# Loading and transposing the first x chunk in halves, and moving gate values through DRAM, in a fused attention and FFN kernel

## The chip, the cores and the metric

The kernel runs on one core of a Trainium2 chip. The metric is the device time of one execution in microseconds (us). "Span" is the time from the first to the last instruction of the profiled execution; the device time is 1.7 to 1.9 us longer in nearly all executions. PE is TensorE (its matmuls), DVE is VectorE, ACT is ScalarE, POOL is GpSimd, and SP is SyncE, which only issues DMAs here; ACTq and SPq are DMA issues of those engines.

A ratio is the mean time of one kernel's fast runs over that of the other's of the same rounds. So it is not quite the ratio of the medians that stand beside it.

## The reference, cut to what matters

```python
g = sigmoid((x * gate_w).sum(-1, keepdims=True))     # one gate value per token
a = infini_attention(x, wq, wk, wv, wo, beta)        # 32 heads of 16, four segments of 512 tokens
b = ((relu(x @ W_gate)) * (x @ W_up)) @ W_down       # 1792 hidden features
return g * a + (1 - g) * b
```

x is 2048 x 512 in bf16. Segment s attends within itself and to a memory matrix made from the keys and values of the segments before it. `beta` gives one mixing value per head.

## The kernel before

A Python list scheduler orders about 1400 operations when the program is built. It models the engines with fixed durations and gives every engine one fixed list. On the chip each engine works through its list in order, and waits on semaphores where an operation needs another engine's result. In before SyncE issued nothing from 21.99 to 28.38 us, where a transpose of keys waited for DVE; the loads of x chunk 2 behind it, which read only DRAM and write a place of their own, were issued from 30.96 us on. A tie is broken by random numbers from a seed. So any change of the operations, and any change of the seed, gives another order everywhere.

The parts that the change touches, with cuts marked:

```python
# loads at the start, in this order on two queues
for i, eng in enumerate(("act", "sp", "act", "sp")):          # x tiles: 128 tokens x 512 features each
    load(eng, [f"hT{i}"], V.hT[:, i, :], x0[:, i, :], 1 << 17)
...  # wq, wk, wv in quarters of 128 KB; wq0 and wq2 on act
load("act", ["gwb"], V.gwb[:], gate_w.partition_broadcast(128), 1 << 17)   # gate weight, fifth on act's queue

# constants from beta, on act and dve
cst = [act(... V.eb = exp(V.braw) ...)]
cst.append(dve(... V.romgh = V.eb + 1 ...))
cst.append(dve(... V.epsv = V.romgh * EPS ...))
...  # eight column fills of vaug from romgh

# gate of segment 0: product on pool, sum and exponential on act
for t in range(4):
    pool(... Tn[t % 2] = hT[t] * gwb ...)
    act(... gl[t] = sum of Tn[t % 2] ...)
act(... gexp = exp(gl) ...)
...
# gate values for the attention's layout: 16 small copies per segment
for a in range(4):
    for jj in range(4):
        ... copy gexp[32*a:32*a+32, 4 tokens] to gexpT[32*jj:32*jj+32, ...]   # on dve or act

# the k mask that an attention matmul ("quad") reads: on dve alone in segment 0
Op([("dve", km, 420)] + ([("act", ka, 720)] if s else []), ...)
```

An attention step is a "quad": matmuls of 32 rows into four banks of PSUM, the memory that matmuls write (`psL`), then one ACT exponential of 128 x 2048 elements into `E`. All quads share those banks, so a quad waits for the exponential of the one before it (0.3 us at B0 in before). PE fills the time between with projections and FFN matmuls. `ek` is an exponential for the keys. The first three bursts of quads are called A0, B0 and C below; 14 matmuls for v stand between A0 and B0 in PE's list.

The softmax here doesn't subtract the row's maximum and nothing guards it: scores larger than these inputs give would overflow.

Of the kernel before, what the change touches and what calls it, by code (L numbers as in the profile page):

```python
# [384 lines left out]
def build_kernel(nc, A_x, A_wq, A_wk, A_wv, A_wo, A_beta, W_g, W_u, W_d, gate_w, out):  # L385
    _, S, D = A_x.shape
    F = W_g.shape[1]
    assert D == 512 and S % 512 == 0 and F % 128 == 0
    NSEG, KT, NF, NT = S // 512, D // 128, F // 128, S // 128
    EPS, SCALE = 1e-6, 16 ** -0.5  # L390
    sc = Sched(seed=59)
    T = {}
    with contextlib.ExitStack() as stack:
        for name, shape, dt in plan(S, D, F):
            T[name] = stack.enter_context(nc.sbuf_tensor(name, shape, dt))
        PL = stack.enter_context(nc.psum_tensor("psL", [128, 4, 512], F32))
        PA = [stack.enter_context(nc.psum_tensor(f"psA{i}", [128, 512], F32)) for i in range(4)]
        for st in sc.streams:
            sc.sem[st] = stack.enter_context(nc.semaphore(f"s_{st}"))
        program(sc, nc, T, PL, PA, A_x, A_wq, A_wk, A_wv, A_wo, A_beta, W_g, W_u, W_d, gate_w, out, NSEG, KT, NF, NT, EPS, SCALE)  # L400
        with nc.Block() as block:
            sc.emit(block)
    return sc


def program(sc, nc, T, PL, PA, A_x, A_wq, A_wk, A_wv, A_wo, A_beta, W_g, W_u, W_d, gate_w, out, NSEG, KT, NF, NT, EPS, SCALE):
# [26 lines left out]
    def xt(c):  # L433
        return [f"xT{c}_{kt}" for kt in range(KT)] if c else [f"xT0_{i}" for i in range(4)]
# [6 lines left out]
    for i, eng in enumerate(("act", "sp", "act", "sp")):  # L441
        load(eng, [f"hT{i}"], V.hT[:, i, :], x0[:, i, :], 1 << 17)
    for nm, w, src in (("wq", V.wq, A_wq), ("wk", V.wk, A_wk), ("wv", V.wv, A_wv)):
        for kt in range(KT):
            load("act" if nm == "wq" and kt % 2 == 0 else "sp", [f"{nm}{kt}"], w[:, kt, :], src[kt * 128:(kt + 1) * 128, :], 1 << 17)
# [63 lines left out]
    xps, xcs = [warm(6, 512, 0, 3)], []  # L509
    for i in range(4):  # L510
        def fx(e, i=i):
            for kt in range(KT):
                ins = e.matmul(PL[:, i, kt * 128:(kt + 1) * 128], lhsT=V.hT[:, i, kt * 128:(kt + 1) * 128], rhs=V.ident[:], start=True, stop=True)
            return ins
        xps.append(pe(fx, 430, reads=[f"hT{i}", "ident"], writes=[f"bankL{i}"], name=f"xt{i}"))
        dst = V.xT[:, :, i * 128:(i + 1) * 128]
        srcp = PL[:, i, :].rearrange("q (k t) -> q k t", k=KT)
        if i % 2 == 0:
            xcs.append(dve(lambda e, d=dst, s_=srcp: e.tensor_copy(d, s_), t_dve(512), reads=[f"bankL{i}"], writes=[f"xT0_{i}"], name=f"xc{i}"))
        else:  # L520
            xcs.append(act(lambda e, d=dst, s_=srcp: e.activation(d, s_, ACT.Copy), t_act(512), reads=[f"bankL{i}"], writes=[f"xT0_{i}"], name=f"xc{i}"))
    xps.append(warm(7, 128, 1, 0))
    sc.queue(0, xps)
# [6 lines left out]
    for s2 in range(2):  # L530
        for tt in range(4):
            cst.append(dve(lambda e, s2=s2, tt=tt: e.tensor_copy(V.vaug[:, s2, tt, :, 16], V.romgh[:, :]), 190, reads=["romgh"], writes=[f"vone{s2}_{tt}"], name="vone"))
# [4 lines left out]
    gq = {"pe": [], "act": [], "dve": [], "flex": [], "pool": [], "sp": []}  # L537
    for c in range(NSEG):
        t0, t1 = 4 * c, 4 * c + 4
        gx = V.gexp[:, t0:t1]  # L540
        if c == 0:
            for t in range(4):
                gq["pool"].append(pool(lambda e, t=t: e.tensor_tensor(V.Tn[:, t % 2, :], V.hT[:, t, :], V.gwb[:], ALU.mult), 1250, reads=[f"hT{t}", "gwb"], writes=[f"Tn{t % 2}"], name=f"gml{t}"))  # L543
                gq["act"].append(act(lambda e, t=t: e.activation(V.Tn[:, t % 2, :], V.Tn[:, t % 2, :], ACT.Copy, accum_out=V.gl[:, t:t + 1]), t_act(512, False) + 100, reads=[f"Tn{t % 2}"], writes=[f"Tn{t % 2}", f"gl{t}"], name=f"gad{t}"))
        else:
            for t in range(t0, t1):
                ld = dma("sp", lambda e, t=t: e.dma_start(V.osb[:, 2, :], A_x[0, t * 128:(t + 1) * 128, :]), 1 << 17, writes=["osb2_0", "osb2_1"], name=f"ldxr{t}")
                ld.after = GATE_T[c] + 4000.0 * (t - t0)
                gq["sp"].append(ld)
                gq["dve"].append(dve(lambda e, t=t: e.tensor_tensor_reduce(out=V.osb[:, 2, :], in0=V.osb[:, 2, :], in1=V.gwb[:], scale=1.0, scalar=0.0, op0=ALU.mult, op1=ALU.add, accum_out=V.gl[:, t:t + 1]),  # L550
                                     t_dve(512) + 70, reads=["osb2_0", "osb2_1", "gwb"], writes=["osb2_0", "osb2_1", f"gl{t}"], name=f"gate{t}"))
# [4 lines left out]
        gexpT_r[c] = []  # L556
        for a in range(4):
            for jj in range(4):
                dst = V.gexpT[32 * jj:32 * jj + 32, 16 * c + 4 * a:16 * c + 4 * a + 4]
                gq["flex"].append(sc.add(Op([("dve", lambda e, a=a, dst=dst, t0=t0, t1=t1: e.tensor_copy(dst, V.gexp[32 * a:32 * a + 32, t0:t1]), 200),  # L560
                                             ("act", lambda e, a=a, dst=dst, t0=t0, t1=t1: e.activation(dst, V.gexp[32 * a:32 * a + 32, t0:t1], ACT.Copy), 215)],
                                            reads=[f"gexp{c}"], writes=[f"gexpT{c}_{a}{jj}"], name="gexpT")))
                gexpT_r[c].append(f"gexpT{c}_{a}{jj}")
# [8 lines left out]
    sc.queue(2, gq["flex"])  # L572
# [15 lines left out]
    def proj(s):  # L588
# [3 lines left out]
        def pj(w, col, name, wname, tokmajor=False):  # L592
            ep = Epoch("proj")

            step = 1 if s == 0 and name == "q" and col < 2 else 2
            for k0 in range(0, KT, step):
# [7 lines left out]
                pes.append(pe(fn, mm(512, step), reads=[f"{wname}{kt}" for kt in range(k0, k0 + step)] + xt(s), name=f"{name}{s}_{col}", ep=ep, role="w2" if k0 else "w"))  # L604
            return ep
        for G in range(4):
            ep = pj(V.wq, G, "q", "wq")
            qs = qslot(s, G)
            evs.append(dve(lambda e, ep=ep, qs=qs: e.tensor_copy(V.qT[:, qs, :], A(ep)[:, :]), t_dve(512), writes=[f"qT{qs}"], name=f"qcp{s}_{G}", ep=ep, role="r"))  # L609
# [3 lines left out]
            evs.append(dve(lambda e, ep=ep, G=G: e.tensor_copy(V.kT[:, G, :], A(ep)[:, :]), t_dve(512), writes=[f"kT{G}"], name=f"kcp{s}_{G}", ep=ep, role="r"))  # L613
            for p in range(2):
# [3 lines left out]
                evs.append(sc.add(Op([("dve", km, 420)] + ([("act", ka, 720)] if s else []), reads=[f"kT{G}", "pm"], writes=[f"kp{ks}"], name=f"kmask{s}_{G}_{p}")))  # L618
# [7 lines left out]
        if s == 0:  # L626
            pes = [p for k in "qkv" for p in pes if p.name[0] == k]
            pes[:2 * KT] = [pes[h * KT + kt] for kt in range(KT) for h in range(2)]
        return pes, evs, sbs, acts, sps

    def va(s):
        return [f"va{s % 2}_{tt}" for tt in range(4)] + [f"vone{s % 2}_{tt}" for tt in range(4)]
# [210 lines left out]
    put(pproj=a, dproj=b, dsb=c_, aphi=d, spk=e_)  # L843
# [89 lines left out]
```

## Time and profile before

| | before |
|---|---|
| device time, median of the first 3 runs | 273.07 us |
| span of the profiled execution | 271.2 us |
| PE / DVE / ACT busy | 97% / 76% / 75% |
| first k matmul, A0, B0, C start | 9.82, 13.94, 17.80, 20.83 us |
| last matmul starts | 268.60 us |

The page's first part gives the busy times of the engines:

```profile
PE 263.0 (97%) x2108; PEld 115.1 (42%) x2143; DVE 204.8 (76%) x382; ACT 203.7 (75%) x210; POOL 99.5 (37%) x156
```

The timeline of the start. Columns: start, busy time, engine, line, operation, out<-in, count; in brackets the idle time of that engine before it, and what ended it.

```profile
3.78 1.89 PE L513 MATMUL psL<-ident,hT 128*128 128x128 bf16 x16 [0.22 <-DMA hT<-in_A_x_dram]
...
6.36 3.63 PE L602 MATMUL psA<-xT,wq 128*128 128x512 bf16 x16
...
9.82 3.62 PE L602 MATMUL psA<-xT,wk 128*128 128x512 bf16 x15
...
11.34 0.19 ACT L544 ACTIVATION_READ_ACCUMULATOR Tn<-Tn 128x1 f32 x1
11.43 0.21 ACT L527 ACTIVATE eb<-braw 128x32 f32<-128x32 bf16 x1
11.67 0.24 DVE L528 TENSOR_SCALAR romgh<-eb 128x32 f32<-128x32 f32 x1 [0.96 <-ACT eb L527]
11.84 0.68 DVE L613 CAST kT<-psA 128x512 bf16<-128x512 f32 x1
...
13.55 0.60 DVE L616 TENSOR_SCALAR kp<-kT,pm 128x512 bf16<-128x512 bf16 x2
...
13.94 0.39 PE L698 MATMUL psL<-qT,kp 32*128 32x512 bf16 x4 [0.51 <-DVE kp L616]
```

PE waits 0.51 us for the first k mask. DVE was late with it, because it had waited 0.96 us for `eb`, and `eb` stood on ACT right behind a gate sum.

The chain of waits of the same stretch. Columns: start, length, what the chain passed through.

```profile
2.68 5.68 DMA gwb<-in_gate_w_dram
...
8.51 4.49 POOL Tn L543 x4
...
13.02 0.73 ACT Tn L544 x2
...
14.01 0.20 ACT gexpT L561
...
14.93 1.06 ACT ek L584
15.98 1.77 ACT E L703
17.76 0.05 issue
17.80 0.40 PE psL L698 x8
```

It says what PE's list of waits doesn't. The load of the gate's weight lands at 8.36. POOL's four products follow it, then ACT's sums, the gate copies, an exponential for the keys (`ek`), and only then the first attention exponential. B0 waits for that.

### The profile page before, as it was taken

The page shows a single profiled execution, that of the slowest core. Times are in us where ns is not written, and L with a number is a line of the kernel's source. Part 1 is how long each engine was busy: PE and PEld are TensorE (multiplying, and loading weights), DVE is VectorE, ACT ScalarE, POOL GpSimd, SP SyncE. Part 2 cuts the span into 40 slices and gives each one's busy share as a digit, 9 for nine tenths or more (in the row PEclk, how much of TensorE's full clock was granted, in tenths as well). Part 3 has the DMA queues.
Part 4 walks back from the last instruction along what each step waited for, and adds up shares of the span by engine and source line. Part 5 has one row for each costly group of instructions (what it writes and reads, how often), then busy time and mean ns, then how long its engine had stood idle before and what let it go on. Part 6 is the DMA issues. An engine that isn't in the chain of part 4 may idle for free.

```text
span 271.2 us, 5268 instructions
## 1 busy us (share of the span) xinstructions
PE 263.0 (97%) x2108; PEld 115.1 (42%) x2143; DVE 204.8 (76%) x382; ACT 203.7 (75%) x210; POOL 99.5 (37%) x156
## 2 busy tenths in 40 slices
PE   8989999999999999999999999999999999999996
PEld 4433343444444444444343444343434444344444
DVE  4689988899889799999888887877773547776300
ACT  3499998898989987899768779887776768682122
POOL 5614343454533253643333532333333242421000
PEclk9999999999999999999999999999999999999999
DMA  6999953102200143210001220000012000000011
GB/s 192 331 365 238 237 96 69 29 7 55 55 25 19 31 89 97 60 39 2 0 2 39 62 78 22 19 2 1 2 39 52 27 19 22 0 0 4 0 39 41
DMA packets 31017, 17.01 MB, mean 63 GB/s; under 512 B 20880, under 2 KB 30992, under 8 KB 30992
## 3 DMA queue, kind: packets, MB, share of 16 engines
q1 hardware_dynamic: 30272, 16.01, 23.3%
q10 hardware_dynamic: 720, 0.66, 1.0%
q8 instruction: 17, 0.28, 0.4%
q14 instruction: 8, 0.07, 0.1%
HBM read 9.84 MB, written 2.10 MB: 44 GB/s over the span
## 4 chain that ended last, share of the span: by engine, by line
PE 88%; ACT 2%; DVE 2%; DMA 2%; issue 2%; POOL 2%; ACTq 1%; DVEq 0%; POOLq 0%
PE psA L780 36%; PE psA L819 17%; PE psL L698 9%; PE psA L602 8%; PE psA L724 7%; PE psA L812 5%; PE psA L600 4%; DMA gwb<-in_gate_w_dram 2%; POOL Tn L543 2%; PE psA L672 1%; PE psA L643 1%; ACT E L703 1%; ACTq L439 1%; DVE osb L828 1%; PE psA L659 0%
## 5 line engine op out<-in xcount | busy, mean ns | idle before, releaser
L703 ACT ACTIVATE E<-psL 128x2048 bf16<-128x2048 f32 x80 | 150.0, 1875 | 31.1 <-PE psL L698 30.6
L706 POOL TENSOR_SCALAR_AFFINE_SELECT E<-E 128x512 bf16<-128x512 bf16 x128 | 85.4, 685 | 139.6 <-ACT E L703 139.5
L780 PE MATMUL psA<-xT,wg 128*128 128x512 bf16 x213 | 58.0, 380 | 1.1 <-issue 0.8
L780 PE MATMUL psA<-xT,wu 128*128 128x512 bf16 x217 | 58.4, 380 | 0.6 <-issue 0.3
L819 PE MATMUL psA<-wd,hT 128*128 128x512 bf16 (+2 forms) x233 | 53.0, 367 | 0.8 <-issue 0.8
L791 DVE TENSOR_TENSOR hT<-psA,rl 128x512 bf16<-128x512 f32 x56 | 38.2, 683 | 13.5 <-PE psA L780 12.5
L698 PE MATMUL psL<-qT,kp 32*128 32x384 bf16 (+3 forms) x512 | 31.7, 301 | 0.8 <-DVE kp L616 0.5
L780 PEld LDWEIGHTS psA<-xT,wu 128*128 128x128 bf16 x224 | 20.4, 98 | 25.8 <-issue 3.2
L819 PEld LDWEIGHTS psA<-wd,hT 128*128 128x128 bf16 x238 | 20.9, 98 | 23.8 <-issue 4.0
L780 PEld LDWEIGHTS psA<-xT,wg 128*128 128x128 bf16 x224 | 20.1, 98 | 24.9 <-issue 3.1
L729 DVE STREAM_TRANSPOSE Tn<-psA 128x512 f32<-128x512 f32 x32 | 20.9, 692 | 7.9 <-PE psA L724 7.9
L789 DVE TENSOR_SCALAR rl<-psA 128x512 bf16<-128x512 f32 x30 | 20.6, 688 | 4.0 <-PE psA L780 3.0
L698 PEld LDWEIGHTS psL<-qT,kp 32*128 32x128 bf16 x512 | 8.9, 92 | 34.0 <-ACT E L703 14.0
L788 ACT ACTIVATE rl<-psA 128x512 bf16<-128x512 f32 x26 | 15.5, 595 | 10.3 <-PE psA L780 10.2
L724 PE MATMUL psA<-E,vaug 128*17 128x256 bf16 (+3 forms) x512 | 20.2, 300 | 0.0
L829 ACT ACTIVATE osb<-psA,omg 128x512 bf16<-128x512 f32 (+2 forms) x10 | 6.4, 645 | 13.7 <-PE psA L812 13.1
L812 PE MATMUL psA<-wo,oT 128*128 128x512 bf16 (+2 forms) x64 | 15.9, 366 | 0.3 <-issue 0.2
L602 PE MATMUL psA<-xT,wk 128*128 128x512 bf16 x62 | 15.9, 380 | 0.2 <-DVE ttmp L585 0.2
L602 PE MATMUL psA<-xT,wq 128*128 128x512 bf16 x61 | 15.5, 380 | 0.5 <-issue 0.3
L600 PE MATMUL psA<-wv,xT 128*128 128x512 bf16 x61 | 14.7, 380 | 0.4 <-issue 0.3
L724 PEld LDWEIGHTS psA<-E,vaug 128*17 128x17 bf16 x512 | 10.7, 90 | 9.4 <-issue 2.5
L609 DVE CAST qT<-psA 128x512 bf16<-128x512 f32 x16 | 10.7, 676 | 3.4 <-PE psA L602 3.3
(71 smaller groups left out, 233.0 us busy)
## 6 DMA issues: line engine op xcount, KB each, us to landing
out_dram<-osb SPq DMA_DIRECT2D x15, 128.0 KB, 1.7
wg<-in_B_W_gate_dram SPq DMA_DIRECT2D x8, 224.0 KB, 5.4
wu<-in_B_W_up_dram SPq DMA_DIRECT2D x8, 224.0 KB, 5.7
wd<-in_B_W_down_dram SPq DMA_DIRECT2D x1, 1792.0 KB, 10.5
osb<-in_A_x_dram SPq DMA_DIRECT2D x12, 128.0 KB, 2.0
wk<-in_A_wk_dram SPq DMA_DIRECT2D x4, 128.0 KB, 5.6
wv<-in_A_wv_dram SPq DMA_DIRECT2D x4, 128.0 KB, 4.9
wo<-in_A_wo_dram SPq DMA_DIRECT2D x1, 512.0 KB, 5.0
```

The costliest lines, as they stand in the source:

```text
L600: ins = e.matmul(A(ep)[:, :], lhsT=V.xT[:, kt, tok + col * 128:tok + (col + 1) * 128], rhs=w[:, kt, :], start=(kt == 0), stop=(kt == KT - 1))
L602: ins = e.matmul(A(ep)[:, :], lhsT=w[:, kt, col * 128:(col + 1) * 128], rhs=V.xT[:, kt, tok:tok + 512], start=(kt == 0), stop=(kt == KT - 1))
L698: ins = q.matmul(PL[:, jj, o:o + w], lhsT=V.kp[32 * jj:32 * jj + 32, kslot(s, n), 128 * j:128 * j + 128], rhs=V.qT[32 * jj:32 * jj + 32, q ...
L703: acts.append(act(lambda a, e=e: a.activation(V.E[:, e, :, :], PL[:, :, :], ACT.Exp, scale=SCALE), t_act(2048), reads=[f"bankL{b}" for b i ...
L706: pools.append(pool(lambda g, ap=ap: g.affine_select(out=ap, in_=ap, compare_op=ALU.is_ge, fill=0.0, base=0, pattern=[[0, 4], [1, 128]], c ...
L724: ins = q.matmul(A(ep)[32 * jj:32 * jj + 17, c:512], lhsT=V.vaug[:, s % 2, j, 8 * G + 2 * jj + p, :], rhs=V.E[:, e, jj, o:o + w], start=(j ...
L729: ds.append(dve(lambda e, p=p, ep=eps[p]: e.transpose(V.Tn[:, p, :], A(ep)[:, :]), t_dve(512), writes=[f"Tn{p}"], name=f"tr{s}_{G}_{p}", e ...
L780: ins = e.matmul(A(ep)[:, :], lhsT=w[:, kt, f * 128:(f + 1) * 128], rhs=V.xT[:, kt, c * 512:(c + 1) * 512], start=(kt == 0), stop=(kt == K ...
L789: ("dve", lambda e, ep=eg, r=r: e.tensor_scalar(V.rl[:, r, :], A(ep)[:, :], 0.0, None, ALU.max), t_dve(512))],
L791: evs.append(dve(lambda e, ep=eu, r=r, hs=hs: e.tensor_tensor(V.hT[:, hs, :], A(ep)[:, :], V.rl[:, r, :], ALU.mult), t_dve(512), reads=[f" ...
L812: ins = e.matmul(A(ep)[:, 0:c1 - c0], lhsT=V.oT[:, o0 + G, i * 128:(i + 1) * 128], rhs=V.wo[:, G, c0:c1], start=st_ and G == 0, stop=sp_ a ...
L819: ins = e.matmul(A(ep)[:, 0:c1 - c0], lhsT=V.hT[:, slots[f], i * 128:(i + 1) * 128], rhs=V.wd[:, f, c0:c1], start=st_ and f == f0, stop=sp ...
```

## The change

Its intent is an earlier start: half of x's features are transposed and projected while the other half is loading. It also takes the small copies of gate values off ACT and DVE (64 copies), moves the constants from beta out of the way, turns eight column fills into one, and allows ACT to make the first k masks. The seed is new. The diff, cut to its core:

```diff
-    sc = Sched(seed=59)
+    sc = Sched(seed=178)
-    for i, eng in enumerate(("act", "sp", "act", "sp")):
-        load(eng, [f"hT{i}"], V.hT[:, i, :], x0[:, i, :], 1 << 17)
+    def load_x0(h):
+        for b, eng in ((0, "act"), (2, "sp")):
+            load(eng, [f"xr{b}_{h}"], V.hT[:, XS + b:XS + b + 2, 256 * h:256 * h + 256], x0[:, b:b + 2, 256 * h:256 * h + 256], 1 << 17)
+    for h in range(2):
+        load_x0(h)
+        for kt in (2 * h, 2 * h + 1):
+            load_w("wq", V.wq, A_wq, kt, "act" if kt % 2 == 0 else "sp")
 ...  (warm-up, 4 x 4 transposes and copies become 2 x 4 x 2, fillers between the halves)
+    cst[0].after = 20000.0          # eb
+    cst[2].after = 40000.0          # epsv
-    for s2 in range(2): for tt in range(4): ... V.vaug[:, s2, tt, :, 16] <- V.romgh
+    ... V.vaug[:, :, :, :, 16] <- V.romgh broadcast, one instruction
-        for a in range(4):
-            for jj in range(4): ... copy of gexp to gexpT, 32 partitions x 4
+        gq["sp"].append(dma("sp", ... gscr[c] <- gexp ...))              # write to DRAM
+        grd = dma("sp", ... [gexpT[32*j:32*j+32] <- gscr[c] for j in range(4)] ...)   # four reads
-            step = 1 if s == 0 and name == "q" and col < 2 else 2
+            early = s == 0 and name == "q" and col < 3                   # three q groups interleaved
-  ... ([("act", ka, 720)] if s else []) ...
+  ... ([("act", ka, 720)] if s or G == 0 else []) ...                    # k mask may go to act
```

More of the change, by code (lines that the diff above doesn't have):

```diff
@@ L433, in xt @@
     def xt(c):
-        return [f"xT{c}_{kt}" for kt in range(KT)] if c else [f"xT0_{i}" for i in range(4)]
+        return [f"xT{c}_{kt}" for kt in range(KT)] if c else [f"xT0_{i}_{h}" for i in range(4) for h in range(2)]
+    XS = 16
     lact, lsp = [], []
@@ L440, in program, with load_w @@
     x0 = A_x[0, 0:512, :].rearrange("(i p) d -> p i d", p=128)
-    for i, eng in enumerate(("act", "sp", "act", "sp")):
-        load(eng, [f"hT{i}"], V.hT[:, i, :], x0[:, i, :], 1 << 17)
-    for nm, w, src in (("wq", V.wq, A_wq), ("wk", V.wk, A_wk), ("wv", V.wv, A_wv)):
+    def load_x0(h):
+        for b, eng in ((0, "act"), (2, "sp")):
+            load(eng, [f"xr{b}_{h}"], V.hT[:, XS + b:XS + b + 2, 256 * h:256 * h + 256], x0[:, b:b + 2, 256 * h:256 * h + 256], 1 << 17)
+    def load_w(nm, w, src, kt, eng="sp"):
+        load(eng, [f"{nm}{kt}"], w[:, kt, :], src[kt * 128:(kt + 1) * 128, :], 1 << 17)
+    for h in range(2):
+        load_x0(h)
+        for kt in (2 * h, 2 * h + 1):
+            load_w("wq", V.wq, A_wq, kt, "act" if kt % 2 == 0 else "sp")
+    for nm, w, src in (("wk", V.wk, A_wk), ("wv", V.wv, A_wv)):
         for kt in range(KT):
-            load("act" if nm == "wq" and kt % 2 == 0 else "sp", [f"{nm}{kt}"], w[:, kt, :], src[kt * 128:(kt + 1) * 128, :], 1 << 17)
+            load_w(nm, w, src, kt)
     load("act", ["gwb"], V.gwb[:], gate_w.partition_broadcast(128), 1 << 17)
@@ L507, in warm, with fx @@
         return pe(fn, m * n * (0.834 if k == 0 else 0.5), writes=[f"bankL{b}"], name=f"warm{k}")
-    xps, xcs = [warm(6, 512, 0, 3)], []
-    for i in range(4):
-        def fx(e, i=i):
-            for kt in range(KT):
-                ins = e.matmul(PL[:, i, kt * 128:(kt + 1) * 128], lhsT=V.hT[:, i, kt * 128:(kt + 1) * 128], rhs=V.ident[:], start=True, stop=True)
-            return ins
-        xps.append(pe(fx, 430, reads=[f"hT{i}", "ident"], writes=[f"bankL{i}"], name=f"xt{i}"))
-        dst = V.xT[:, :, i * 128:(i + 1) * 128]
-        srcp = PL[:, i, :].rearrange("q (k t) -> q k t", k=KT)
-        if i % 2 == 0:
-            xcs.append(dve(lambda e, d=dst, s_=srcp: e.tensor_copy(d, s_), t_dve(512), reads=[f"bankL{i}"], writes=[f"xT0_{i}"], name=f"xc{i}"))
-        else:
-            xcs.append(act(lambda e, d=dst, s_=srcp: e.activation(d, s_, ACT.Copy), t_act(512), reads=[f"bankL{i}"], writes=[f"xT0_{i}"], name=f"xc{i}"))
-    xps.append(warm(7, 128, 1, 0))
-    sc.queue(0, xps)
+    xps, xcs = [[warm(7, 512, 0, 3)], []], []
+    for h in range(2):
+        if h == 1:
+            xps[0].append(warm(6, 128, 1, 0))
+        for i in range(4):
+            def fx(e, i=i, h=h):
+                for kt in (2 * h, 2 * h + 1):
+                    ins = e.matmul(PL[:, i, kt * 128:(kt + 1) * 128], lhsT=V.hT[:, XS + i, kt * 128:(kt + 1) * 128], rhs=V.ident[:], start=True, stop=True)
+                return ins
+            xps[h].append(pe(fx, 115 if h else 215, reads=[f"xr{i & 2}_{h}", f"hT{XS + i}", "ident"], writes=[f"bankL{i}"], name=f"xt{i}"))
+            dst = V.xT[:, 2 * h:2 * h + 2, i * 128:(i + 1) * 128]
+            srcp = PL[:, i, 256 * h:256 * h + 256].rearrange("q (k t) -> q k t", k=2)
+            if i % 2 == 0:
+                xcs.append(dve(lambda e, d=dst, s_=srcp: e.tensor_copy(d, s_), t_dve(256), reads=[f"bankL{i}"], writes=[f"xT0_{i}_{h}"], name=f"xc{i}"))
+            else:
+                xcs.append(act(lambda e, d=dst, s_=srcp: e.activation(d, s_, ACT.Copy), t_act(256), reads=[f"bankL{i}"], writes=[f"xT0_{i}_{h}"], name=f"xc{i}"))
     sc.queue(0, [t for t in xcs if t.eng == "dve"])
@@ L529, in program @@
     cst.append(dve(lambda e: e.tensor_scalar(V.epsv[:], V.romgh[:], EPS, None, ALU.mult), 190, reads=["romgh"], writes=["epsv"], name="epsv"))
-    for s2 in range(2):
-        for tt in range(4):
-            cst.append(dve(lambda e, s2=s2, tt=tt: e.tensor_copy(V.vaug[:, s2, tt, :, 16], V.romgh[:, :]), 190, reads=["romgh"], writes=[f"vone{s2}_{tt}"], name="vone"))
+    cst.append(dve(lambda e: e.tensor_copy(V.vaug[:, :, :, :, 16].rearrange("q s t h -> q (s t) h"), V.romgh[:, :].unsqueeze(1).to_broadcast([128, 8, 32])), 420, reads=["romgh"], writes=["vone"], name="vone"))
+    cst[0].after = 20000.0
+    cst[2].after = 40000.0
     sc.queue(0, [t for t in cst if t.eng == "act"])
@@ L536, in program @@
     gexpT_r = {}
-    gq = {"pe": [], "act": [], "dve": [], "flex": [], "pool": [], "sp": []}
+    gscr = nc.dram_tensor("gscr", [NSEG, 4, 32, 4], F32).ap()
+    gq = {"pe": [], "act": [], "dve": [], "pool": [], "sp": []}
     for c in range(NSEG):
@@ L542, in program @@
             for t in range(4):
-                gq["pool"].append(pool(lambda e, t=t: e.tensor_tensor(V.Tn[:, t % 2, :], V.hT[:, t, :], V.gwb[:], ALU.mult), 1250, reads=[f"hT{t}", "gwb"], writes=[f"Tn{t % 2}"], name=f"gml{t}"))
+                gq["pool"].append(pool(lambda e, t=t: e.tensor_tensor(V.Tn[:, t % 2, :], V.hT[:, XS + t, :], V.gwb[:], ALU.mult), 1250, reads=[f"xr{t & 2}_0", f"xr{t & 2}_1", f"hT{XS + t}", "gwb"], writes=[f"Tn{t % 2}"], name=f"gml{t}"))
                 gq["act"].append(act(lambda e, t=t: e.activation(V.Tn[:, t % 2, :], V.Tn[:, t % 2, :], ACT.Copy, accum_out=V.gl[:, t:t + 1]), t_act(512, False) + 100, reads=[f"Tn{t % 2}"], writes=[f"Tn{t % 2}", f"gl{t}"], name=f"gad{t}"))
@@ L555, in program @@
         gq["dve"].append(dve(lambda e, om=om: e.reciprocal(om, om), 250, reads=[f"omg1{c}"], writes=[f"omg{c}"], name="omg"))
-        gexpT_r[c] = []
-        for a in range(4):
-            for jj in range(4):
-                dst = V.gexpT[32 * jj:32 * jj + 32, 16 * c + 4 * a:16 * c + 4 * a + 4]
-                gq["flex"].append(sc.add(Op([("dve", lambda e, a=a, dst=dst, t0=t0, t1=t1: e.tensor_copy(dst, V.gexp[32 * a:32 * a + 32, t0:t1]), 200),
-                                             ("act", lambda e, a=a, dst=dst, t0=t0, t1=t1: e.activation(dst, V.gexp[32 * a:32 * a + 32, t0:t1], ACT.Copy), 215)],
-                                            reads=[f"gexp{c}"], writes=[f"gexpT{c}_{a}{jj}"], name="gexpT")))
-                gexpT_r[c].append(f"gexpT{c}_{a}{jj}")
+        gexpT_r[c] = [f"gexpT{c}"]
+        gq["sp"].append(dma("sp", lambda e, c=c, gx=gx: e.dma_start(gscr[c].rearrange("a r t -> (a r) t"), gx), 2048, reads=[f"gexp{c}"], writes=[f"gscr{c}"], name=f"gwr{c}"))
+        gdst, gsrc = V.gexpT[:, 16 * c:16 * c + 16], gscr[c].rearrange("a r t -> r a t")
+        grd = dma("sp", lambda e, gdst=gdst, gsrc=gsrc: [e.dma_start(gdst[32 * j:32 * j + 32, :].rearrange("r (a t) -> r a t", t=4), gsrc) for j in range(4)], 8192, occ=2000.0, reads=[f"gscr{c}"], writes=[f"gexpT{c}"], name=f"grd{c}")
+        grd.nd = 4
+        gq["sp"].append(grd)
     def c2g(s):
@@ L571, in program @@
     sc.queue(1, gq["dve"])
-    sc.queue(2, gq["flex"])
     sc.queue(3, gq["sp"])
@@ L592, in pj @@
         def pj(w, col, name, wname, tokmajor=False):
-            ep = Epoch("proj")
-            step = 1 if s == 0 and name == "q" and col < 2 else 2
+            early = s == 0 and name == "q" and col < 3
+            ep = Epoch("att" if early else "proj")
+            step = 1 if early else 2
             for k0 in range(0, KT, step):
@@ L603, in fn, with cp @@
                     return ins
-                pes.append(pe(fn, mm(512, step), reads=[f"{wname}{kt}" for kt in range(k0, k0 + step)] + xt(s), name=f"{name}{s}_{col}", ep=ep, role="w2" if k0 else "w"))
+                pes.append(pe(fn, mm(512, step), reads=[f"{wname}{kt}" for kt in range(k0, k0 + step)] + (xt(s) if not early else [f"xT0_{i}_{k0 // 2}" for i in range(4)]), name=f"{name}{s}_{col}", ep=ep, role="w2" if k0 else "w"))
             return ep
+        def cp(s, dst, ep, **k):
+            alts = [("dve", lambda e: e.tensor_copy(dst(), A(ep)[:, :]), t_dve(512))]
+            if False:
+                alts.append(("act", lambda e: e.activation(dst(), A(ep)[:, :], ACT.Copy), t_act(512)))
+            return sc.add(Op(alts, ep=ep, role="r", **k))
         for G in range(4):
@@ L608, in proj @@
             qs = qslot(s, G)
-            evs.append(dve(lambda e, ep=ep, qs=qs: e.tensor_copy(V.qT[:, qs, :], A(ep)[:, :]), t_dve(512), writes=[f"qT{qs}"], name=f"qcp{s}_{G}", ep=ep, role="r"))
+            evs.append(cp(s, lambda qs=qs: V.qT[:, qs, :], ep, writes=[f"qT{qs}"], name=f"qcp{s}_{G}"))
             if s > 0 and G % 2:
@@ L612, in proj @@
             ep = pj(V.wk, G, "k", "wk")
-            evs.append(dve(lambda e, ep=ep, G=G: e.tensor_copy(V.kT[:, G, :], A(ep)[:, :]), t_dve(512), writes=[f"kT{G}"], name=f"kcp{s}_{G}", ep=ep, role="r"))
+            evs.append(cp(s, lambda G=G: V.kT[:, G, :], ep, writes=[f"kT{G}"], name=f"kcp{s}_{G}"))
             for p in range(2):
@@ L617, in proj @@
                 ka = lambda e, G=G, p=p, ks=ks: e.activation(V.kp[:, ks, :], V.kT[:, G, :], ACT.Copy, scale=V.pm[:, p:p + 1])
-                evs.append(sc.add(Op([("dve", km, 420)] + ([("act", ka, 720)] if s else []), reads=[f"kT{G}", "pm"], writes=[f"kp{ks}"], name=f"kmask{s}_{G}_{p}")))
+                evs.append(sc.add(Op([("dve", km, 420)] + ([("act", ka, 720)] if s or G == 0 else []), reads=[f"kT{G}", "pm"], writes=[f"kp{ks}"], name=f"kmask{s}_{G}_{p}")))
             if s < NSEG - 1 and G % 2:
@@ L627, in proj @@
             pes = [p for k in "qkv" for p in pes if p.name[0] == k]
-            pes[:2 * KT] = [pes[h * KT + kt] for kt in range(KT) for h in range(2)]
+            pes[:3 * KT] = [pes[h * KT + kt] for kt in range(KT) for h in range(3)]
         return pes, evs, sbs, acts, sps
     def va(s):
-        return [f"va{s % 2}_{tt}" for tt in range(4)] + [f"vone{s % 2}_{tt}" for tt in range(4)]
+        return [f"va{s % 2}_{tt}" for tt in range(4)] + ["vone"]
     def mu(s):
@@ L842, in program @@
     a, b, c_, d, e_ = proj(0)
-    put(pproj=a, dproj=b, dsb=c_, aphi=d, spk=e_)
+    put(pproj=a[3 * KT:], dproj=b, dsb=c_, aphi=d, spk=e_)
+    sc.queue(0, xps[0] + a[:3] + xps[1] + a[3:3 * KT])
     slots = None
```

## The prediction

> **What bounds the kernel.** The page gives PE 97% busy of 271.2 us, DVE 76%, ACT 75%. The view of PE's waits finds about 5 us idle in all; after 22 us no wait is over 0.2 us, and the table by stretches has PE 98 to 100% busy from 22 to 268 us. The steady part is a fixed amount of TensorE issue. Only the head (0 to 22 us) has slack; the tail isn't touched.
>
> **The head, from the timeline.** Six warm-up matmuls from 0.84; x landed 3.73 to 4.52; 16 transposes from 3.78, 107 ns apart; seven fillers; q matmuls from 6.36, 216 ns apart; k from 9.82 to 13.4; then 0.5 us idle until the first attention matmul at 13.94 (released by DVE's k mask), and 0.3 us near 17.5 (released by ACT's exponential). [...]
>
> **What the change does.**
> 1. x in halves. The first transposes still wait for the first landing (estimate 3.8 to 4.0). Then 8 transposes (0.85 us), six fillers (0.64) and three q matmuls from about 5.5; those run at half clock (0.6 us lost), while the second 8 transposes run faster (0.4 won). I expect k to start at 9.6 to 10.1: nearly no gain.
> 2. Constants from beta. DVE's first k eviction started at 11.84 although its matmuls were issued by 10.7: it stood in order behind `romgh`, which waited for `eb`, and that for the beta load (landed 11.1). Deferring them, and k masks allowed on ACT, should put the first attention matmul near 12.5. Worth 0.5 to 1 us. Three q groups that end together queue 0.69 us copies on DVE, which takes some back.
> 3. Gate replication. 64 copies of 0.20 us (57 on ACT) become 4 writes and 16 small reads through DRAM. In segment 0, four of them (0.89 us) stood before `ek` and the first exponential (15.89), which should now start near 13. Later, PE doesn't wait for ACT or DVE, so the other 10 us are worth about nothing. The values are first used at 38.9, so the longer path fits. The risk is SyncE: it issues in order, and a wait for gate values holds back the loads of x chunk 1 (landed 24.3, used from 26.8).
> 4. Eight column fills (0.23 us, DVE, 22 to 25 us) become one; not on PE's path.
> 5. A new seed reorders everything: plus or minus 0.5 us.
>
> **Sum.** Halves 0 (within 0.3), constants and first exponential minus 0.8, reordering minus 0.3: **272.0 us**, range 270.7 to 273.0. Chances: faster by over 2% 0.02, within 2% 0.96, slower by over 2% 0.02.
>
> **What would show it.** Step 1: k starts at 9.6 to 10.1, first three q matmuls 427 ns apart. Step 2: first attention matmul near 12.5; PE idle in 10 to 22 us under half of before's 1.1 us. Step 3: ACT busy down by about 11 us, DVE by 1 to 3; PE busy from 30 to 250 us unchanged within 0.5; first exponential near 13. PE's last matmul moves by no more than the head did.
>
> **What would make it wrong.** A clock released earlier (up to 0.6 us more gain); SyncE blocked so that PE waits for x chunk 1 (1 to 3 us slower); DVE's copies holding PSUM banks so that PE idles in 10 to 16 us; another count of swaps between kinds of matmul.

(Before's trace does show: matmuls of 512 columns started 427 ns apart in the warm-up, and 216 ns apart from 6.36 us on. Step 1's 0.6 us lost is an estimate from this, three matmuls at 0.21 us each; the 0.4 won is eight transposes at half of their 107 ns. 273.07 less 0, 0.8 and 0.3 is 271.97, put down as 272.0.)

## The result, and the profile after

After ran in 273.01 us (272.89 to 273.51, 6 runs), before in 273.01 (272.66 to 273.2, 6 runs). The ratio is 1.0004, with a 95% interval of 0.9991 to 1.0017: no change. A second series of after on another occasion gave 273.56 against 273.05 for before, ratio 1.0018 (1.0007 to 1.003).

The engines' busy times:

```profile
PE 263.2 (97%) x2107; PEld 114.2 (42%) x2143; DVE 199.9 (74%) x365; ACT 195.1 (72%) x160; POOL 97.9 (36%) x156
```

ACT lost 8.6 us of work and DVE 4.9 us; PE and the span (271.1) stayed. The timeline of the start:

```profile
3.78 1.06 PE L527 MATMUL psL<-ident,hT 128*128 128x128 bf16 x8
...
5.36 0.82 PE L612 MATMUL psA<-xT,wq 128*128 128x512 bf16 x3
...
6.01 0.61 PE L527 MATMUL psL<-ident,hT 128*128 128x128 bf16 x8
...
9.38 3.62 PE L612 MATMUL psA<-xT,wk 128*128 128x512 bf16 x15
...
10.69 1.31 DVE L617 CAST kT<-psA 128x512 bf16<-128x512 f32 x2
...
11.92 0.85 DVE L631 TENSOR_SCALAR kp<-kT,pm 128x512 bf16<-128x512 bf16 x1
...
12.65 0.63 ACT L557 ACTIVATE Tn<-Tn 128x512 f32<-128x512 f32 x1 [0.39 <-POOL Tn L556]
...
13.28 0.71 ACT L632 ACTIVATE kp<-kT,pm 128x512 bf16<-128x512 bf16 x1
...
14.04 0.40 PE L713 MATMUL psL<-qT,kp 32*128 32x512 bf16 x4 [1.04 <-ACT kp L632]
...
14.94 1.85 ACT L718 ACTIVATE E<-psL 128x2048 bf16<-128x2048 f32 x1
```

The k matmuls start 0.44 us earlier, and the first k eviction on DVE comes at 10.69 instead of 11.84, as the change meant. But A0 starts at 14.04, later than in before, and PE's wait there has doubled to 1.04 us. The list of operations shows why: the scheduler put the mask that A0 reads on ACT, behind the fourth gate sum, and put the other mask, not needed until later, on DVE. The chain of waits:

```profile
2.87 5.09 DMA gwb<-in_gate_w_dram
...
8.13 4.50 POOL Tn L556 x4
...
12.65 0.72 ACT Tn L557 x2
13.38 0.62 ACT kp L632
14.00 0.05 issue
14.04 0.40 PE psL L713 x4
```

It begins as before's chain does (weight, products, gate sums), but in before it reached only B0; now A0 itself hangs on it.

### The profile page after: what moved, and what is told of

It reads as the page before. It is cut to its first block, busy times and chain, and to the rows that moved or that the text cites. A ratio compares the mean times of both kernels' runs of the same rounds, so it can differ in the third digit from the quotient of the medians.

```text
span 271.1 us, 5223 instructions
## 1 busy us (share of the span) xinstructions
PE 263.2 (97%) x2107; PEld 114.2 (42%) x2143; DVE 199.9 (74%) x365; ACT 195.1 (72%) x160; POOL 97.9 (36%) x156
## 4 chain that ended last, share of the span: by engine, by line
PE 93%; DMA 2%; POOL 2%; issue 1%; ACTq 1%; ACT 1%; POOLq 0%
PE psA L795 36%; PE psA L834 18%; PE psL L713 10%; PE psA L612 8%; PE psA L739 7%; PE psA L610 5%; PE psA L827 5%; DMA gwb<-in_gate_w_dram 2%; POOL Tn L556 2%; PE psA L658 1%; PE psA L687 1%; ACTq L441 1%; PE psA L674 0%; ACT Tn L557 0%; ACT kp L632 0%
## 5 line engine op out<-in xcount | busy, mean ns | idle before, releaser
L721 POOL TENSOR_SCALAR_AFFINE_SELECT E<-E 128x512 bf16<-128x512 bf16 x128 | 83.5, 671 | 138.8 <-ACT E L718 138.6
L795 PE MATMUL psA<-xT,wg 128*128 128x512 bf16 x217 | 58.6, 380 | 0.9 <-issue 0.8
L795 PE MATMUL psA<-xT,wu 128*128 128x512 bf16 x212 | 57.0, 380 | 1.1 <-issue 0.6
L834 PEld LDWEIGHTS psA<-wd,hT 128*128 128x128 bf16 x238 | 21.5, 98 | 23.5 <-issue 2.3
L803 ACT ACTIVATE rl<-psA 128x512 bf16<-128x512 f32 x30 | 17.9, 598 | 14.2 <-PE psA L795 13.7
L804 DVE TENSOR_SCALAR rl<-psA 128x512 bf16<-128x512 f32 x26 | 17.9, 687 | 5.7 <-PE psA L795 5.3
L844 ACT ACTIVATE osb<-psA,omg 128x512 bf16<-128x512 f32 (+2 forms) x11 | 7.1, 648 | 15.2 <-PE psA L827 13.1
L612 PE MATMUL psA<-xT,wq 128*128 128x512 bf16 x62 | 16.5, 380 | 0.2
L640 DVE CAST vaug<-psA 128x512 bf16<-128x512 f32 x16 | 10.9, 688 | 2.9 <-PE psA L610 2.9
```

What stands on the lines that cost most here:

```text
L612: ins = e.matmul(A(ep)[:, :], lhsT=w[:, kt, col * 128:(col + 1) * 128], rhs=V.xT[:, kt, tok:tok + 512], start=(kt == 0), stop=(kt == KT - 1))
L721: pools.append(pool(lambda g, ap=ap: g.affine_select(out=ap, in_=ap, compare_op=ALU.is_ge, fill=0.0, base=0, pattern=[[0, 4], [1, 128]], c ...
L795: ins = e.matmul(A(ep)[:, :], lhsT=w[:, kt, f * 128:(f + 1) * 128], rhs=V.xT[:, kt, c * 512:(c + 1) * 512], start=(kt == 0), stop=(kt == K ...
L803: evs.append(sc.add(Op([("act", lambda e, ep=eg, r=r: e.activation(V.rl[:, r, :], A(ep)[:, :], ACT.Relu), t_act(512)), ("dve", lambda e, e ...
L834: ins = e.matmul(A(ep)[:, 0:c1 - c0], lhsT=V.hT[:, slots[f], i * 128:(i + 1) * 128], rhs=V.wd[:, f, c0:c1], start=st_ and f == f0, stop=sp ...
```

## The experiments

The order of the operations is a confounder: any edit gives another one. So the program got a second pass. It takes a recorded order of all operations, with each one's engine and PSUM bank, and places them again, deriving every wait anew. With no edit it reproduced before and after instruction for instruction. In the experiments "in the order of before" or "of after" means this; only what is named differs.

**Theory G:** the start hangs on one chain (load of the gate's weight, four products on POOL, sums on ACT, and whatever stands behind them in ACT's list), and after the start nothing that the change does matters. **Rivals:** D, the start hangs on DVE's copies and on beta's constants, as predicted; S, later stretches absorb what the start wins; O, the new order costs it.

All marks, read from the traces (starts in us; "weight" is the landing of the gate's weight; the last two columns are the time from C, and from the first k matmul, to the start of the last matmul; kernels in the order of after have 8 FFN matmuls ahead of C, those in the order of before 10):

| kernel | order | k | weight | A0 | first exp. | B0 | C | C to last | k to last |
|---|---|---|---|---|---|---|---|---|---|
| before | before | 9.82 | 8.36 | 13.94 | 15.89 | 17.80 | 20.83 | 247.77 | 258.78 |
| after | after | 9.38 | 7.96 | 14.04 | 14.94 | 17.50 | 20.09 | 248.41 | 259.12 |
| e8 (after again) | after | 10.09 | 8.69 | 14.79 | 15.68 | 18.24 | 20.84 | 248.41 | 259.16 |
| e1 | after | 9.39 | 8.07 | 12.94 | 15.04 | 16.95 | 19.65 | 248.41 | 258.68 |
| e2 | after | 9.70 | 7.70 | 13.24 | 13.69 | 16.70 | 19.89 | 248.41 | 258.60 |
| e5 | after | 10.26 | 8.29 | 13.81 | 14.26 | 17.27 | 19.86 | 248.65 | 258.25 |
| e9 | after | 10.23 | 13.27 | 19.34 | 20.23 | 24.46 | 27.06 | 248.41 | 265.24 |
| e10 | after | 11.32 | 8.33 | 14.87 | 15.31 | 18.32 | 20.92 | 248.41 | 258.01 |
| e3 | before | 9.84 | 8.89 | 13.74 | 16.43 | 18.34 | 21.37 | 247.77 | 259.30 |
| e6 | before | 10.47 | 8.38 | 14.02 | 15.94 | 17.86 | 20.88 | 247.77 | 258.18 |
| e7 | before | 10.20 | 8.66 | 14.26 | 15.15 | 17.71 | 20.74 | 247.77 | 258.31 |
| e4 | before | 9.98 | 8.16 | 13.53 | 14.66 | 16.99 | 20.01 | 247.77 | 257.80 |
| e11 | before | 10.98 | 7.88 | 14.53 | 14.97 | 17.98 | 21.01 | 247.77 | 257.80 |
| e12 | before | 11.11 | 7.71 | 14.66 | 15.11 | 18.12 | 21.14 | 247.77 | 257.80 |
| e13 | before | 9.99 | 8.69 | 13.54 | 14.23 | 16.99 | 20.02 | 248.00 | 258.03 |
| e14 | before | 10.16 | 8.50 | 13.71 | 14.15 | 17.16 | 20.19 | 247.88 | 257.91 |

How to read it: the column "C to last" is nearly constant for each order. Whatever the experiment does to ACT and DVE, the last 248 us change by 0.24 us at most (e5, e13 and e14; 0 in the others), so the end is decided by the time of C. Where PE has no wait, A0 comes 3.55 us after the first k matmul, because it stands behind all 16 k matmuls in PE's list. The column "k to last" has to be read with care: a late k makes it shorter, since waits for the gate's chain then pass while PE is still busy with k. The weight, in its old place in ACT's queue, landed at 7.70 to 8.89 us in twelve traces (all but e9 to e12).

### e1: the first two k masks change engines

```diff
 # order of after
-kmask0_0_0 on act, kmask0_0_1 on dve
+kmask0_0_0 on dve, kmask0_0_1 on act
```

> The kernel after, in its own order of all instructions, but the first two k masks change engines: the one that the first attention matmul reads goes to DVE, the other to ACT. Theory H (the head's gain was given back because that mask stood on ACT behind the gate sums): first attention matmul from 14.04 to about 12.9 us; the second attention matmul then waits for the first exponential, which stays behind mask and phi exponential on ACT, so it moves only from 17.5 to about 16.9; total 0.5 to 0.7 us under after, about 272.4. Rival S (later stretches absorb whatever the head wins, or the loss is the new order's alone): the first matmul moves as well, but the total stays within 0.15 us of after, 273.0.

Measured: 272.69 us (272.07 to 272.81, 5 runs), before 272.82 (9 runs), ratio 0.9992 (0.998 to 1.0005). A0 came at 12.94 and PE's 1.04 us wait in front of it went. Its chain of waits shows the next releaser:

```profile
12.75 0.72 ACT Tn L587 x2
13.47 0.61 ACT kp L662
14.09 0.10 ACT gexp L595
14.18 0.95 ACT ek L624
15.13 1.77 ACT E L748
16.90 0.05 issue
16.95 0.40 PE psL L743 x8
```

The other mask and `ek` now stand before the first exponential. It started at 15.04, as it would have without the edit, and B0 waited 0.5 us for it. So H is right about the mask and about the next wait (B0 at 16.95, expected 16.9). S is not: from C to the last matmul it takes as long as in after, to 0.01 us. Of the 0.5 to 0.7 us expected in the total, the profiles show 0.44 (last matmul at 268.06 instead of 268.50), and the rounds can't tell that from nothing.

### e2: and the first exponential goes first on ACT

```diff
 # order of after, with e1's edit; act's list
-gad3, kmask0_0_1, gexp, kexp0_1, exp0_0A0
+gad3, gexp, exp0_0A0, kmask0_0_1, kexp0_1
```

(`gad` is a gate sum, `gexp` the gate's exponential, `kexp` the one for the keys, which the profile lists as `ek`, and `exp0_0A0` is the attention exponential of A0.)

> As e1, and on ACT the first exponential goes ahead of the second k mask and the first phi exponential. Theory H: first exponential starts near 13.7 instead of 14.94, second attention matmul near 16.3 instead of 17.5, first FFN matmul near 17.1 instead of 18.27, total about 1.1 us under after, 271.9. Rival S: total within 0.15 us of after.

Measured: 272.69 us (272.6 to 273.32, 5 runs), before 272.82, ratio 1.0003 (0.9991 to 1.0016). The expected 271.9 was a miss. The first exponential came at 13.69 as expected and B0 at 16.70, but C didn't follow. It waited 0.5 us for B0's exponential (PE's list of waits), because the mask and both key exponentials now stood in front of that one. Besides, k began 0.32 us later than in after's first profile. So the 0.5 us that e1 had in front of B0 reappeared in front of C, behind the next items of ACT's list.

### e3: only the constants from beta move, in the order of before

```diff
 # order of before
-act: gad1, eb, gad2, ...       dve: qcp0_3, romgh, kcp0_0, epsv, kcp0_1, ...
+act: gad1, gad2, ..., eb, exp0_0B0   dve: qcp0_3, kcp0_0, kcp0_1, ..., romgh, epsv, vone
```

> The kernel before, in its own order, but the three small constants from beta leave their place ahead of the k evictions and come near 17 to 22 us. The prediction's step 2 by itself: first attention matmul near 12.9 instead of 13.94, total 0.5 to 1 us under before, 272.0 to 272.5. Theory H (the next wait takes over): the first attention matmul moves to about 13.0, but the first exponential stays at 15.9 behind the gate sums, four gate copies and the phi exponential on ACT, the second attention matmul stays at 17.8, and the total stays within 0.2 us of before, 273.0.

Measured: 273.02 us (272.39 to 273.44, 5 runs), before 272.82, ratio 1.0006 (0.9992 to 1.002). This is the prediction's deferring of the constants by itself, and it is worth nothing. A0 did come nearer to k (3.90 us after it instead of 4.12), but at 13.74, not at the 12.9 or 13.0 expected. DVE was free for the two masks at 12.38, and they took 1.57 us:

```profile
12.38 1.57 DVE L646 TENSOR_SCALAR kp<-kT,pm 128x512 bf16<-128x512 bf16 x2
```

Taken singly, the first mask took 1.30 us and the second 0.34. The first one ended 0.15 us after POOL's last product, which ran from 12.37 to 13.53. The same shows in seven traces (after, e8, e1, e3, e4, e13, e14): a mask that DVE starts during POOL's last product lasts 0.45 to 1.30 us and ends 0.15 us after that product. (In e2 and e5 the mask starts within 0.17 us of the product's end and takes the usual 0.34.) So the gate's chain reaches A0 through DVE too. And the first exponential stayed 7.54 us behind the weight's landing (7.53 in before), and B0 9.45 behind it (9.44).

### e4: the whole change in the order of before

```diff
 # all parts of the change
-order and seed of after
+order of before for every operation that both have; both first k masks on dve
```

> All parts of the change (x in halves, three q groups interleaved, gate values through DRAM, late constants, one column fill), but every instruction that both kernels have keeps the order and the engine that it had before, so both first k masks stay on DVE; no new seed. Theory H: k starts at 9.4, first attention matmul near 12.9, first exponential near 14.7, second attention matmul near 16.6, first FFN matmul near 17.4 (before 18.74), total 1.0 to 1.3 us under before, about 271.9. Rival S: total 273.0 within 0.2. If it comes out between (272.4 to 272.7), part of the head's gain is lost later whatever the order.

Measured: 272.31 us (272.08 to 272.74, 5 runs), before 272.82, ratio 0.9986 (0.9973 to 1.0). After the first k matmul PE waits for nothing; from 3 us to 260 us its list of waits has one line, for x:

```profile
PE psL L557 <- DMA hT<-in_A_x_dram: 0.4, 1, 0.4
```

From the first k matmul to the last matmul it takes 257.80 us: 0.98 less than in before, 1.32 less than in after. The start won nothing here (k at 9.98, not 9.4), so the expected 271.9 was missed. The total says that the change holds about half a microsecond, which after's own placement and order hide; the interval reaches 1.0, so this run alone is at the edge of the noise.

### e5: ACT's list is cleared at the start, in the order of after

```diff
 # order of after; act's list
-gad3, kmask0_0_0, gexp, kexp0_1, exp0_0A0, kexp0_3, exp0_0B0, exp0_0C
+exp0_0A0, kmask0_0_1, gad3, exp0_0B0, gexp, kexp0_1, exp0_0C, kexp0_3
 # dve: kmask0_0_0 instead of kmask0_0_1; omg1 and omg a few places later
```

> The kernel after in its own order, but on ACT the first three attention exponentials go ahead of the gate's last sum and exponential and of both phi exponentials, and the first k mask is on DVE. Measure: time from the first k matmul to PE's last matmul, which leaves out what clock and landings do to the start. It was 258.78 us in before, 259.12 in after, 258.67 in e1, 258.60 in e2, 257.80 in e4 (which had no wait after k). Theory A (PE's waits in ACT's in-order queue in the first 20 us are the whole loss): 257.8 to 258.0 here too, total near 272.2. Rival O (the new order of after costs time later on): 258.4 or more here, because only e4 had the old order.

Measured: 273.03 us (272.76 to 273.45, 5 runs), before 273.05, ratio 0.9994 (0.9981 to 1.0007). The expected 272.2 was a miss. In three of its five executions the device time is 2.3 to 2.5 us longer than the span; its spans have a median of 271.0 us against 271.3 for before. k began late, at 10.26. From k to C no wait is left (9.60 us). From k to the last matmul it is 258.25 us, between what A (257.8 to 258.0) and O (258.4 or more) expected. Of that, 0.24 us is a wait that the edit makes later (C to last is 248.65 instead of 248.41), and the new order itself costs about 0.21. That number is worked out from the table: 248.41 less two FFN matmuls of 0.216 us each is 247.98, against 247.77 in the order of before.

### e6: only the halves of x, in the order of before

```diff
 # before, with the x load, transposes and first three q groups of after; all else as in before
```

> The kernel before in its own order, with x in halves and three q groups interleaved, and nothing else. Theory A: k starts at 9.4 to 10.0 (before 9.82), but the first attention matmul stays at 13.7 to 14.0 behind the beta constants and the second near 17.8 behind ACT, so the total stays within 0.2 us of before. If the halves are worth what they win at the start of k, the total is 0.1 to 0.4 under before.

Measured: 272.89 us (272.48 to 273.06, 5 runs), before 273.05, ratio 0.9992 (0.998 to 1.0004). k began at 10.47, later than in before: PE waited 0.6 us for the second halves of x, which landed at 6.78 and 7.04. Yet A0 came at 14.02 and B0 at 17.86, where they were anyway. The end doesn't hang on the start of k here, as A expected.

### e7: only the gate values through DRAM, in the order of before

```diff
-64 copies gexp -> gexpT on act or dve
+4 x (write gexp to DRAM, 4 reads into gexpT) on sp
```

> The kernel before in its own order, with the 64 gate copies replaced by writes and reads through DRAM, and nothing else. Theory A: of the 13 us of ACT and DVE time only the four copies ahead of the first exponential count: it starts near 15.0 instead of 15.89, the second attention matmul near 17.1 instead of 17.8, total about 0.5 us under before, 272.4. The prediction had this part at nothing beyond the head; a rival is that ACT's relief later counts too, then 1 us or more under before.

Measured: 272.74 us (272.36 to 273.66, 6 runs), before 273.05, ratio 0.9996 (0.998 to 1.0011). ACT's busy time fell from 203.7 to 192.5 us. The first exponential moved from 7.53 to 6.49 us behind the weight's landing. B0, expected at 17.1, came only at 17.71: it follows A0 by 3.45 us, with the 14 v matmuls between, and A0 had waited 0.4 us for DVE's mask, behind beta's constants as in before. So e3 leaves the wait ahead of B0 (1.1 us, and 0.3 of the one ahead of A0), and e7 the wait ahead of A0; only e4 removes both. And from C to the last matmul it takes 247.77 us, as in before to the hundredth: eleven microseconds less work on ACT are worth nothing once the start is over. The 0.5 us expected in the total doesn't stand out of the rounds.

### e8: after once more

> The kernel after once more, unchanged, for a second profile of its start. Theory: the first k matmul's time varies between executions with the release of the clock and the landing of x (9.38, 9.39, 9.70, 9.98 in four kernels with this start); first attention matmul at 14.0 within 0.2 whatever k does, because it waits for the gate sums on ACT; total within 0.2 us of before.

Measured: 273.56 us (273.37 to 273.92, 5 runs), before 273.05, ratio 1.0018 (1.0007 to 1.003), so slower than expected. The last half of x landed at 6.66 us instead of 5.74, k began at 10.09, and the weight landed 0.73 us later than in the first profile. A0 came 0.75 us later, at 14.79 (the expectation had 14.0), and everything behind it shifted with it. A0 follows the weight's landing by 6.08 us in one profile and 6.10 in the other; it follows k by 4.66 and 4.70. As both starts moved together, these two profiles can't tell by their times which of them A0 hangs on, though PE's list of waits names ACT's mask in both (1.0 and 1.1 us). e9 does.

### e9: the gate's weight is loaded later

```diff
 # order of after; act's list
-ldxr0_1, ldwq2, ldgwb, ..., xc3
+ldxr0_1, ldwq2, ..., xc3, ldgwb
```

> The kernel after in its own order, but the load of the gate's weight (128 KB) is issued by ACT after its last copy of transposed x, about 4.5 us later than in after. In all kernels so far the first attention exponential starts a fixed time after that load lands (after 6.98 and 6.99 us in two profiles; 7.53, 7.54, 7.57 in the three that keep the four gate copies). Theory G (the chain weight load, four products on POOL, sums on ACT in order, k mask or exponential, sets the head): landing near 11.3, first attention matmul at landing plus 6.1, first exponential at landing plus 7.0, total about 2.5 us over after (275.5 to 276.5). Rival D (DVE's copies and beta set it): total within 0.5 us of after.

Measured: 280.42 us (279.65 to 281.17, 4 runs), before 273.18, ratio 1.0263 (1.0242 to 1.0284). The load landed at 13.27, two microseconds later than I had expected. A0 followed it by 6.07 us and the first exponential by 6.96 (in after 6.08 and 6.98). The total is 4 us above the expected range. PE's list of waits (engine, tile and line; what it waited for; us in total, times, longest), and the end of the chain:

```profile
PE psL L743 <- ACT kp L662: 5.5, 1, 5.5
```

```profile
13.44 4.49 POOL Tn L586 x4
...
17.95 0.72 ACT Tn L587 x2
18.67 0.62 ACT kp L662
...
19.34 0.61 PE psL L743 x4
19.95 4.58 PE psA L640 x14
```

D is out: a load of 128 KB that serves only gate values first used near 40 us sets the kernel's time. The last line shows a second cost. The 14 v matmuls took 4.58 us, and 3.13 in after's chain. PE had idled for 5.5 us, and the trace shows half the clock: matmuls came 427 ns apart, and 216 ns from 22.84 us on. Its clock record has the half clock from 16.02 to 22.85 us; the last k matmul had ended at 13.85, 2.2 us before. The mean granted clock was 0.988 in this profile, and 1.000 in all the others. After's record has the half clock as well from 271.16 us on, 2.4 us behind its last matmul, and before's from 272.59, 3.8 us behind. So the pause is the likely cause; why its length differs, no run tells.

With POOL's products out of the way, DVE's mask (the other one, at the same place of DVE's list as in after) took 0.34 us; in after it took 0.85 and in e8 0.89, beside the products:

```profile
12.77 0.34 DVE L661 TENSOR_SCALAR kp<-kT,pm 128x512 bf16<-128x512 bf16 x1
```

### e10: the gate's weight is loaded one place earlier

```diff
 # order of after; act's list
-ldwq0, ldxr0_1, ldwq2, ldgwb
+ldwq0, ldxr0_1, ldgwb, ldwq2
```

> The kernel after in its own order, but the load of the gate's weight is issued one place earlier on ACT, ahead of the third quarter of wq. Theory G: it lands 0.3 to 0.7 us earlier relative to the x and wq loads; first exponential at landing plus 7.0; time from first k matmul to the last matmul 258.4 to 258.8 instead of 259.12 and 259.16; total 0.3 to 0.7 us under after, 272.5 to 273.0. Rival D: 259.1 stays.

Measured: 273.54 us (272.68 to 274.35, 6 runs), before 273.18, ratio 1.0012 (0.9995 to 1.0029). From k to the last matmul it took 258.01 us, less than expected, but this is no gain of the edit: the weight landed at 8.33, no earlier than in after (7.96). k began at 11.32, because PE waited 1.3 us for x and 0.4 us for wq, whose last quarter landed at 9.07 instead of 6.38; with k so late, A0's mask was ready in time, and A0 came 3.55 us after k. Of theory G, e10 tests only the first exponential, which came 6.98 us after the landing, as expected.

### e11 and e12: the same in the order of before, with halves and with whole rows of x

```diff
 # e4's parts and order; act's list
-ldwq2, ldgwb        kexp0_1, exp0_0A0
+ldgwb, ldwq2        exp0_0A0, kexp0_1
 # e12: besides, x load, transposes and q projections as in before
```

> All parts of the change in the order of before (as e4), the gate's weight one place earlier, and on ACT the first attention exponential ahead of the first phi exponential. Theory G: PE waits for nothing after the first k matmul, 257.8 us from there to the last matmul as in e4; total 272.2 (within 0.25), about 0.8 us under before; faster than e4 only by rounds in which the weight lands late.

> As e11, but with the x load, transposes and q projections of before (whole rows, two groups interleaved). Theory: the first k matmul came at 9.82, 9.84 and 10.20 with whole rows and at 9.38 to 10.47 (mean 9.90 of seven) with halves, because the second halves land in the stretch of 5 to 7 us[...]; so total within 0.2 us of e11. If the halves win what the change intended, e12 is 0.3 us or more slower than e11.

Measured: e11 273.2 us (272.82 to 273.67), ratio 1.0 (0.9988 to 1.0012); e12 273.32 (272.94 to 273.51), ratio 1.0003 (0.9991 to 1.0015); 5 runs each, before 273.18. e11's 272.2 was a miss, though the 257.80 us from k on came true in both: k began at 10.98 and 11.11, too late for the gate's chain to hold anything up. e12's timeline shows PE waiting for wq:

```profile
7.01 1.02 PE L629 MATMUL psA<-xT,wq 128*128 128x512 bf16 x4 [1.31 <-DMA wq<-in_A_wq_dram]
8.51 2.76 PE L629 MATMUL psA<-xT,wq 128*128 128x512 bf16 x12 [0.48 <-DMA wq<-in_A_wq_dram]
```

Halves and whole rows are equal here.

### e13 and e14: the weight in its old place, with whole rows and with halves

```diff
 # e12 and e11; act's list
-ldgwb, ldwq2
+ldwq2, ldgwb
```

> The start of before (whole rows of x, two q groups interleaved, the gate's weight after wq on ACT's queue), with gate values through DRAM, late constants and one column fill, in the order of before, and on ACT the first attention exponential ahead of the first phi exponential. Theory G: first k matmul at 9.8 to 10.2 as in the other kernels with whole rows, 257.8 us from there to the last matmul, total 0.6 to 1.0 us under before. If the halves are what e4 won by, it is at before's time within 0.2.

> As e13 with x in halves and three q groups interleaved, so e4 with the first exponential moved up. First k matmul at 9.4 to 10.5, 257.8 us from there to the last matmul, total within 0.3 us of e13. If the halves are worth what they were meant to win (k 0.4 us earlier as in the first profile of after), it is 0.4 us under e13.

Measured: e13 272.3 us (271.94 to 272.42), ratio 0.9978 (0.9964 to 0.9991); e14 272.33 (271.78 to 272.63), ratio 0.998 (0.9968 to 0.9993); 5 runs each, before 272.8. Both are 0.2% faster than before, clear of noise (e13's gain is at the lower end of what was expected). From k to the last matmul they took 258.03 and 257.91 us, not 257.8: a q matmul at 41.7 us came 0.23 and 0.11 us late, for a reason that the list of waits doesn't name. After was level with before or slower in its two series, so they beat it too, though it did not run beside them. Whole rows do as well as halves: none of the gain is theirs. What of it is due to the exponential's new place on ACT, which is not in the change, no run separates; e4 has no wait after k without it. e13's timeline has no wait ahead of A0 or B0:

```profile
9.99 3.62 PE L629 MATMUL psA<-xT,wk 128*128 128x512 bf16 x16
13.54 0.40 PE L725 MATMUL psL<-qT,kp 32*128 32x512 bf16 x4
13.86 3.19 PE L627 MATMUL psA<-wv,xT 128*128 128x512 bf16 x14
16.99 0.40 PE L725 MATMUL psL<-qT,kp 32*128 32x384 bf16 x8
```

## Why the prediction was wrong

The prediction put after at 272.0 us, within 270.7 to 273.0. It measured 273.01, just outside. "Within 2%" was right; the gain of 1 us wasn't there.

**Step 2 failed, and it is most of the cause.** Together with step 3's earlier first exponential it was counted as a gain of 0.8 us; the waits that it was to remove grew by 0.13 us instead (sum below). It said that deferring beta's constants, "and k masks allowed on ACT, should put the first attention matmul near 12.5. Worth 0.5 to 1 us." The first attention matmul came at 14.04 and 14.79. Near 12.5 it could not have come: A0 stands behind the 16 k matmuls in PE's list, so with k at 9.6 to 10.1 it is due at 13.15 at the earliest, as the prediction's own times say (k from 9.82 to 13.4 in before). Deferring did free DVE (first k eviction at 10.69 instead of 11.84), but e3 shows that this alone gains nothing: DVE's mask is held until POOL's last product is done (it took 1.30 us and ended 0.15 us after that product), and the first exponential still comes at the end of the gate's chain. And the freedom to use ACT did harm: A0's mask went behind the gate sums, and PE waited 1.04 us for it instead of 0.51. With both masks on DVE and the gate copies gone (e4), the waits are gone. ACT did not take the mask ahead of the gate sum, though it sat idle for 0.39 us just before that sum. I had read before's wait from the list of waits, which named DVE, and stopped there. The chain of waits of before already named the gate's weight, POOL and ACT.

**Step 1 was about right in size and wrong in its reason.** k was expected at 9.6 to 10.1. With halves and the weight in its old place it came at 9.38 to 10.47 in eight profiles (mean 9.93), with whole rows at 9.82 to 10.20 in four (mean 9.96). The early q matmuls weren't at half clock in after: three took 0.82 us, since the clock record has the full clock there from 4.92 us on (in before from 6.35), a risk that the prediction had named. The late second halves of x take the gain. The DMAs have a slow stretch, which the table by stretches of before shows (columns: stretch, length, busy time of PE, PEld, DVE, ACT and POOL, granted clock, DMA share, GB/s):

```profile
2.50:4.00 1.50, 1.28 (x6) 0.38 (x5) 0.60 (x3) 0.83 (x1) 1.30 (x5) 1.00 1.04 361
4.00:5.50 1.50, 1.50 (x17) 1.50 (x16) 0.91 (x2) 1.05 (x2) 0.49 (x1) 1.00 0.93 283
5.50:7.00 1.50, 1.50 (x12) 0.95 (x11) 0.47 (x1) 0.60 (x1) 0.00 (x0) 1.00 0.81 238
```

As whole rows, all of x has landed by 4.18 to 4.52 us (five profiles), ahead of most of it. As halves, the last piece lands at 5.44 to 7.45 (eleven profiles), in the midst of it. The loads didn't get smaller: x is four loads of 128 KB either way, but the second halves stand third on their queues, behind a quarter of wq. With whole rows wq's first quarters stand third, and they land at 5.88 to 6.92 us (ten loads). So the place in the queue is likely the reason, rather than the halving; no run tells them apart, nor why the DMAs are slow there.

**Step 3** was right that ACT's relief beyond the start is worth nothing: e7 shows 247.77 us from C on, with and without it. ACT's busy time fell by 8.6 us (11 predicted) and DVE's by 4.9 (1 to 3 predicted), since the new order also moved four relus from DVE to ACT; with the order kept (e7) it was 11.2 and 1.8. The first exponential came at 14.94, not near 13, because of the same chain. PE did not wait for x chunk 1, the risk that I had named: SyncE issued its four loads from 15.02 us on, ahead of the first gate write (22.32).

**Step 5**, the new seed, was counted as a gain of 0.3 us, for which the prediction gave no reason. It cost about 0.2 (e5), and its placing of the mask cost more.

The sum, first profile of after against before: start of k -0.44; waits between k and C +0.13 (before 11.01 - 10.03 = 0.98, after 10.71 - 9.60 = 1.11, the smaller numbers being those without waits); new order +0.21. Together -0.10, which is the difference of the last matmuls (268.50 and 268.60). For the second profile it is +0.27, +0.17 and +0.21, so +0.65 (269.25).

## What to carry to other kernels

When one engine is busy 97% of the time, follow its few waits back to their first cause, across engines that look idle: here a small load and a slow product on POOL, needed only near 40 us, stood in ACT's in-order list ahead of what PE needed at once. Giving a scheduler one more engine for a critical operation can put it behind something slower, so look where it was placed. An operation can also be slow because of another engine's work beside it: compare its duration with the same operation elsewhere in the trace (DVE's mask here: 0.34 us, and up to 1.30 beside POOL's products). And separate an edit from the reordering that it causes, by replaying the old order, before judging either.
